# Linear attention and a highway feed-forward on one core: feed-forward in token rows, keys and queries turned in 64-row tiles

## The chip, the core and the metric

The kernel runs on one core of a Trainium2 chip. The metric is the device time of one execution in microseconds. Three executions of the kernel before took 109.54 (median), 109.30 and 109.64 us.

## What is computed

Linear attention with a decay per head, over 4 batches, 8 heads, 768 positions and head size 64, followed by a highway layer over 3,072 tokens of width 512. From the reference (blocks of 64 positions):

```python
intra = einsum('bhic,bhjc->bhij', qb, kb) * Dmask
intra = einsum('bhij,bhjd->bhid', intra, vb)
inter = einsum('bhid,bhde->bhie', qb * lam_pow, kv_state)
out[:, :, sl] = intra + inter
kv_state = lam_block * kv_state + einsum('bhsd,bhse->bhde', kb * rev_pow, vb)
...
H = maximum(x @ w_h, 0);  T = sigmoid(x @ w_t + b_t)
return T * H + (1 - T) * x
```

`x` is the attention output as token rows of 512 features. The inputs and the output are float32.

## The kernel before

A step n is 256 positions of one batch with all heads; there are 12 steps, three per batch, each of two halves b of 128 positions. The decay is folded into queries and values: the query is multiplied by a power of lambda, the value by its inverse, so that the running state `kv`, a PSUM bank, needs no decay.

The order of all work is written out by hand in the string PLAN. Each token names an operation, its step and parts, sometimes an engine (`@ACT`) and the PSUM banks that it takes (`=40`). All engines work through their tokens in that order. The seven banks b0 to b6 each hold one tile at a time; the eighth is `kv`. BUFS gives the number of buffers of each SBUF tile.

For each step: `Lk`, `Lq`, `Lv` load halves of the heads on SyncE's queue (L173), in packets of 512 bytes (two positions of 64 floats). `CK` casts the keys, `CQ` and `CV` scale queries and values (L190); `TK` and `TQ` turn keys and queries in 128x128 transposes (L204), 16 for a step; `EK` and `EQ` copy them out as kT and qT (L101 on ScalarE, L103 on VectorE and GpSimd). `SS` interleaves the scores (L216) with the update of the state (L221); `KE` copies the state out. `M` masks the scores on VectorE (L255). `I` and `A` add state part (L271) and masked part (L281) into a bank bo, whose columns are tokens and whose partitions are features; `D` copies it out as xT.

The feed-forward works on xT with features in the partitions. `F` holds a 128x128 piece of a weight matrix and streams 256 tokens (L300), 32 matmuls for a step, fewer tokens in the last. `H` computes max(h, 0) - x (L305), `G` the sigmoid with the bias as a column (L314), `X` the product th (L318), all with features in the partitions. `R` turns x and th back to token rows in PSUM and adds them there, by matmuls with the identity in 64-row tiles (L347; L327 for the last step), `E` copies the sum out and `ST` stores it (L356, L337). `Z` issues spins, matmuls on zeros that fill waiting time of TensorE in the opening (L366).

The lines that a reader needs for the tile shapes:

```python
T.transpose(t[:, i, j, :], get(x + "b", n)[:, j, h:h + 2, :], id128)                # 128x128
T.matmul(get("x", n, r)[:, b, j, :], lhsT=x[half(r), j, b * C:(b + 1) * C],
         rhs=id128[half(r), half(r)], ...)                                          # 64-row tiles
```

Of the kernel before, what the change touches and what calls it, by code (L numbers as in the profile page):

```python
# [17 lines left out]
Lk.0.0 Lv.0.1 Lv.0.0 Lq.0.0 Lk.0.1 Lq.0.1 Lv.1.1 CK.0.0@POOL Lq.1.0 Z.12=0 TK.0.0=0 Lq.1.1 CV.0.0@DVE Lk.1.0  # L18
CQ.0.0@POOL EK.0.0@DVE Lv.1.0 CV.0.1@DVE CK.0.1@ACT Lk.1.1 Z.11=1 TQ.0.0=1 B=2 EQ.0.0@ACT CQ.0.1@POOL W.0.1 W.0.0
Z.6=0 TQ.0.1=3 TK.0.1=4 EQ.0.1@DVE U.0.0 EK.0.1@ACT W.1.1 S.0.0=56 KE.0.0@DVE S.0.1=01 CQ.1.2@POOL W.1.0 M.0.0.1 Z.1=3  # L20
U.0.1 I.0=34 M.0.1.1 KE.0.1@ACT Lk.2.1 M.0.0.0 A.0.1 M.0.1.0 TQ.1.2=0 Lq.2.1 CV.1.2@DVE CK.1.2@ACT EQ.1.2@ACT Lq.2.0
Z.8=1 TK.1.2=1 A.0.0 EK.1.2@DVE Lk.2.0 D.0.0@DVE Z.3=5 SS.1.1=56 WC.0.0.1@ACT WC.0.0.0@POOL M.1.1.0 KE.1.0@ACT
WC.0.1.0@POOL D.0.1@ACT Lv.2.1 WC.0.1.1@DVE Z.4=0 SS.1.0=01 M.1.1.1 I.1=35 KE.1.1@ACT Lv.2.0 F.0.0.0=4 WC.1.1.0@DVE PT
M.1.0.1 Lk.3.1 F.0.1.0=6 M.1.0.0 WC.1.0.0@POOL WC.1.0.1@ACT Lk.3.0 WC.1.1.1@DVE A.1.1 A.1.0 BC F.0.0.1=1 H.0.1 Lq.3.1
D.1.1@ACT H.0.0 D.1.0@ACT F.0.1.1=0 Lq.3.0 CQ.2.2@POOL F.1.0.0=2 Lv.3.0 G.0.1@ACT CK.2.2@DVE F.1.0.1=6 Lv.3.1
G.0.0@ACT X.0.1@DVE TQ.2.2=5 Lq.4.0 X.0.0@DVE TK.2.2=4 EQ.2.2@ACT CV.2.2@POOL F.1.1.0=3 Lq.4.1 EK.2.2@DVE G.1.0@ACT
H.1.0 SS.2.0=01 Lk.4.1 H.1.1 CK.3.2@POOL SS.2.1=54 Lk.4.0 M.2.0.1 F.1.1.1=2 KE.2.0@ACT M.2.1.0 Lv.4.0 TK.3.2=3 M.2.1.1
CQ.3.2@POOL G.1.1@ACT I.2=15 M.2.0.0 Lv.4.1 A.2.1 X.1.0@DVE A.2.0 Lk.5.0 R.0=40 D.2.0@ACT D.2.1@DVE CV.3.2@POOL
TQ.3.2=6 E.0.0@ACT Lk.5.1 F.2.1.1=1 E.0.1@ACT EQ.3.2@DVE Lq.5.1 EK.3.2@ACT X.1.1@DVE F.2.1.0=5 CQ.4.2@POOL Lq.5.0
R.1=40 H.2.1 SS.3.1=62 Lv.5.0 F.2.0.0=3 CK.4.2@POOL KE.3.0@ACT M.3.1.1 Lv.5.1 E.1.1@ACT M.3.1.0 SS.3.0=52 E.1.0@ACT  # L30
H.2.0 Lq.6.0 TQ.4.2=0 KE.3.1@ACT CV.4.2@POOL M.3.0.1 TK.4.2=6 G.2.1@ACT Lq.6.1 F.2.0.1=4 M.3.0.0 EQ.4.2@ACT EK.4.2@DVE
Lv.6.0 I.3=32 A.3.0 CK.5.2@POOL A.3.1 Lk.6.1 SS.4.1=56 D.3.0@ACT D.3.1@DVE TK.5.2=0 KE.4.0@ACT M.4.1.1 Lk.6.0
F.3.0.0=2 G.2.0@ACT CQ.5.2@POOL EK.5.2@DVE Lv.6.1 SS.4.0=36 H.3.0 F.3.0.1=0 Lq.8.0 M.4.0.0 CV.5.2@POOL M.4.0.1
TQ.5.2=2 Lk.9.0 G.3.0@ACT F.3.1.0=3 X.2.1@DVE Lq.7.0 EQ.5.2@ACT X.2.0@DVE F.3.1.1=6 CQ.6.2@POOL M.4.1.0 Lq.7.1
KE.4.1@ACT I.4=14 H.3.1 G.3.1@ACT R.2=25 Lk.8.1 X.3.0@DVE A.4.0 E.2.1@ACT X.3.1@DVE A.4.1 Lk.7.1 SS.5.0=30 E.2.0@ACT
D.4.0@DVE CK.6.2@POOL SS.5.1=56 D.4.1@ACT Lk.7.0 TQ.6.2=2 M.5.0.0 KE.5.0@ACT CV.6.2@POOL TK.6.2=1 M.5.1.1 Lv.7.0
EQ.6.2@ACT F.4.1.0=4 M.5.0.1 Lv.7.1 EK.6.2@ACT F.4.0.0=3 H.4.1 Lk.8.0 M.5.1.0 I.5=62 SS.6.1=01 H.4.0 Lq.8.1 A.5.0
KE.6.0@ACT M.6.1.0 CQ.7.2@POOL R.3=45 Lv.9.1 A.5.1 M.6.1.1 SS.6.0=30 D.5.0@ACT Lv.8.0 F.4.0.1=1 M.6.0.0 D.5.1@ACT
M.6.0.1 Lk.9.1 TQ.7.2=6 G.4.0@ACT CK.7.2@POOL F.5.0.0=3 Lq.10.1 EQ.7.2@ACT F.4.1.1=2 H.5.0 Lk.10.1 E.3.1@ACT X.4.0@DVE
TK.7.2=0 CV.7.2@POOL G.4.1@ACT I.6=63 ST.0 KE.6.1@DVE F.5.0.1=5 X.4.1@DVE Lv.8.1 F.5.1.0=1 G.5.0@ACT CK.8.2@POOL  # L40
EK.7.2@DVE Lq.9.0 A.6.0 E.3.0@ACT H.5.1 A.6.1 SS.7.1=20 Lq.9.1 D.6.0@ACT D.6.1@DVE TK.8.2=4 M.7.1.1 F.6.1.0=1 Lv.9.0
EK.8.2@ACT X.5.0@DVE CK.9.2@POOL F.6.1.1=6 KE.7.0@DVE Lk.10.0 CQ.8.2@POOL H.6.1 R.4=30 SS.7.0=54 Lk.11.1 E.4.0@ACT
F.5.1.1=1 E.4.1@ACT M.7.0.1 G.6.1@ACT ST.4 M.7.1.0 TK.9.2=3 Lq.10.0 M.7.0.0 TQ.8.2=0 G.5.1@ACT CV.8.2@POOL F.6.0.0=4
EQ.8.2@DVE Lk.11.0 KE.7.1@ACT X.5.1@DVE I.7=25 EK.9.2@ACT Lq.11.0 A.7.0 H.6.0 A.7.1 CQ.9.2@POOL SS.8.0=01 X.6.1@DVE
D.7.1@ACT Lv.10.1 SS.8.1=34 M.8.0.1 D.7.0@ACT F.6.0.1=6 KE.8.0@DVE Lq.11.1 CK.10.2@POOL F.7.0.0=5 M.8.1.0 G.6.0@ACT
M.8.1.1 ST.3 TQ.9.2=1 CV.9.2@POOL H.7.0 F.7.1.0=2 EQ.9.2@ACT Lv.10.0 X.6.0@DVE TK.10.2=3 M.8.0.0 ST.1 I.8=45
EK.10.2@ACT CQ.10.2@POOL H.7.1 SS.9.1=61 A.8.1 KE.9.0@ACT M.9.1.0 A.8.0 R.5=02 M.9.1.1 SS.9.0=36 CK.11.2@POOL
E.5.1@DVE F.7.0.1=1 KE.9.1@ACT M.9.0.1 E.5.0@ACT F.7.1.1=2 D.8.0@DVE D.8.1@ACT ST.5 CQ.11.2@POOL M.9.0.0 G.7.0@ACT
Lv.11.1 TK.11.2=6 Lv.11.0 I.9=04 F.8.1.0=5 EK.11.2@ACT ST.2 X.7.0@DVE TQ.10.2=3 G.7.1@ACT H.8.1 CV.10.2@POOL F.8.0.0=1
EQ.10.2@ACT R.6=65 H.8.0 A.9.1 X.7.1@DVE A.9.0 SS.10.1=31 D.9.0@ACT D.9.1@DVE F.8.1.1=2 E.6.1@ACT M.10.1.1 F.9.1.0=0  # L50
E.6.0@DVE G.8.1@ACT M.10.1.0 ST.6 TQ.11.2=4 CV.11.2@POOL KE.10.0@DVE F.9.1.1=5 EQ.11.2@ACT X.8.1@DVE SS.10.0=16
G.9.1@ACT H.9.1 R.7=32 M.10.0.1 KE.10.1@ACT F.8.0.1=4 X.9.1@DVE E.7.0@ACT M.10.0.0 E.7.1@ACT I.10=06 SS.11.0=53
G.8.0@ACT ST.7 A.10.0 M.11.0.0 A.10.1 SS.11.1=21 D.10.1@ACT X.8.0@DVE F.9.0.0=5 KE.11.0@ACT M.11.1.0 D.10.0@ACT
F.9.0.1=6 M.11.0.1 M.11.1.1 F.10.1.0=4 G.9.0@ACT H.9.0 I.11=20 X.9.0@DVE A.11.0 A.11.1 R.8=31 D.11.0@ACT R.9=56
E.8.0@ACT F.10.0.0=2 E.9.0@DVE E.9.1@ACT E.8.1@ACT D.11.1@DVE ST.9 F.10.1.1=3 H.10.0 ST.8 F.10.0.1=6 H.10.1 G.10.1@ACT
F.12.1.1=5 G.10.0@ACT X.10.1@DVE F.11.1.1=1 F.11.1.0=0 G.12.1@ACT X.10.0@DVE F.11.0.1=2 G.11.1@ACT H.11.1 F.12.1.0=4
R.10=36 G.11.0@ACT H.12.1 X.11.1@DVE F.11.0.0=0 E.10.0@ACT X.12.1@DVE F.12.0.1=4 E.10.1@ACT H.11.0 F.12.0.0=1
G.12.0@ACT X.11.0@DVE ST.10 R.11.1.1=5 H.12.0 R.11.0.2=3 E.11.1.1@DVE X.12.0@DVE E.11.0.2@ACT ST.11.1.1 R.11.1.0=0
ST.11.0.2 E.11.1.0@DVE ST.11.1.0
"""  # L60

BUFS = dict(kf=5, qf=5, vf=5, kb=3, qb=2, vs=3, kT=2, qT=2, m=8, xT4=2, th4=2, xT2=3, xT1=2, th2=2, th1=2, hm2=3, hm1=2, tb2=2, tb1=2, ss=4, o=5, oh=2, oq=1)
# [3 lines left out]
def kernel(  # L66
# [18 lines left out]
    J = 2  # L85
    N = B * NST
# [19 lines left out]
    lam_bc = singles.tile([128, H], F32)  # L106
    A.dma_start(out=lam_bc, in_=lam.partition_broadcast(128))
    bt_r = singles.tile([KC, 128], F32)
    A.dma_start(out=bt_r, in_=moe_b_t.rearrange("(j p) -> j p", p=128))
    id128 = singles.tile([128, 128], BF16)  # L110
    make_identity(nc, id128)
    blank = singles.tile([128, 512], BF16)
    V.memset(blank, 0.0)
    tk_i = singles.tile([128, NST, J], I32)
    P.iota(tk_i, pattern=[[2 * C, NST], [1, J]], base=0, channel_multiplier=J)
    tri = singles.tile([128, J, J, C // J], F32)
    P.memset(tri, 1.0)
    for b in range(2):
        P.affine_select(out=tri[half(b)], in_=tri[half(b)], compare_op=ALU.is_ge, fill=0.0, base=0,
                        pattern=[[-1, J], [1, J], [J, C // J]], channel_multiplier=-J)  # L120
    tri = tri.rearrange("p j i q -> p j (i q)")
    tk_f = singles.tile([128, NST, J], F32)
    V.tensor_copy(tk_f, tk_i)
    id_f = singles.tile([KC, KC], F32)
    V.tensor_copy(id_f, id128[0:KC, 0:KC])
    A.preload_act_table_set("natural_log_exp_and_others")
    ln_bc = singles.tile([128, H], F32)
    A.activation(ln_bc, lam_bc, AF.Ln)
    p_ln = singles.tile([128, NST, H, J], F32)
    V.tensor_tensor(p_ln, in0=ln_bc[:, None, :, None].to_broadcast([128, NST, H, J]),  # L130
                    in1=tk_f[:, :, None, :].to_broadcast([128, NST, H, J]), op=ALU.mult)
    pow_q = singles.tile([128, NST, H, J], F32)
    A.activation(pow_q, p_ln, AF.Exp)
    pow_v = singles.tile([128, NST, H, J], F32)
    A.activation(pow_v, p_ln, AF.Exp, scale=-1.0)
    bt_col = singles.tile([128, KC], F32)
# [4 lines left out]
    kv = ps.tile([128, NP, 128], F32, tag="kv", name="kv", bufs=1)  # L141
    V.memset(kv, 0.0)


    made = {}

    def groups(n, b):
        return ((n,), b) if n < N - 1 else ((n, b), 0)
# [12 lines left out]
    def get(*key):  # L161
        return made[key]
# [7 lines left out]
    def load(x, n, p, eng):  # L170
        b, c = divmod(n, NST)
        hs = heads(p)
        (A if eng else nc.sync).dma_start(out=new((x + "f", n), [128, H, J * D], F32)[:, hs],  # L173
                          in_=SRC[x][b, hs, c * 2 * C:(c + 1) * 2 * C, :].rearrange("h (p j) d -> p h (j d)", j=J))

# [7 lines left out]
    def cast_k(n, p, eng):  # L183
        hs = heads(p)
        copy(eng, new(("kb", n), [128, J, H, D])[:, :, hs].rearrange("p j h d -> p h j d"),
             get("kf", n)[:, hs].rearrange("p h (j d) -> p h j d", j=J))

    def scale(n, p, eng, src, dst, pw):
        z = H if p == 2 else 4
        ENG[eng].tensor_tensor(dst, in0=get(src, n)[:, heads(p)].rearrange("p h (j d) -> p h j d", j=J),  # L190
                               in1=pw[:, n % NST, heads(p), :, None].to_broadcast([128, z, J, D]), op=ALU.mult)

    def cast_q(n, p, eng):
        scale(n, p, eng, "qf", new(("qb", n), [128, J, H, D])[:, :, heads(p)].rearrange("p j h d -> p h j d"), pow_q)

    def cast_v(n, p, eng):
        scale(n, p, eng, "vf", new(("vs", n), [128, H, J, D])[:, heads(p)], pow_v)

# [220 lines left out]
```

## Time and profile before

| | us |
|---|---|
| median of three runs | 109.54 |
| span of the profiled execution, the only time that its record gives | 109.3 |
| TensorE, matmuls busy | 99.4 |
| VectorE busy | 82.7 |
| ScalarE busy | 71.9 |
| GpSimd busy | 55.7 |
| share of the 16 DMA engines, loads and stores | 85.1% |

The span runs from the first to the last instruction. Matmuls overlap, so a busy TensorE need not be at its peak; the chain of waits tells better what a block of matmuls costs. GpSimd's times are rough. Engines wait for each other through semaphores, and the profile names the one that came last.

### The profile page before, as it was taken

How to read it: one execution, taken by the hardware profiler on the slowest of the kernel's cores; microseconds unless marked ns; L12 is line 12 of the kernel's file. 1: busy time of each engine (PE TensorE's matmuls, PEld its weight loads, DVE VectorE, ACT ScalarE, POOL GpSimd, SP SyncE). 2: the span in 40 equal slices, each digit the busy share in tenths (PEclk: the TensorE clock that was granted, in tenths of full speed). 3: DMA queues.
4: the chain of work that ended last, by engine and by line, in shares of the span. 5: the costliest groups of instructions: out<-in, count | busy, mean ns of one | idle time of the engine just before them, and what ended most of it. 6: DMA issues, size and time to landing. Idle time of an engine off the chain costs nothing.

```text
span 109.3 us, 4968 instructions
## 1 busy us (share of the span) xinstructions
PE 99.4 (91%) x2188; PEld 80.6 (74%) x2190; DVE 82.7 (76%) x140; ACT 71.9 (66%) x129; POOL 55.7 (51%) x46
## 2 busy tenths in 40 slices
PE   4986989899999999999999999998999599999950
PEld 1343654688887878889899889896888478899940
DVE  1241595878998696999977989999858958958960
ACT  3304263787866489499579749975696758776940
POOL 6029420427979858959468296499691600000000
PEclk9999999999999999999999999999999999999999
DMA  0899999999999999989999999599999413207264
GB/s 5 233 304 290 291 366 386 312 290 287 290 266 304 287 250 262 302 228 289 296 300 293 305 341 270 181 346 326 321 333 323 170 69 125 73 6 296 94 233 151
DMA packets 42701, 27.59 MB, mean 252 GB/s; under 512 B 1588, under 2 KB 38712, under 8 KB 42680
## 3 DMA queue, kind: packets, MB, share of 16 engines
q1 hardware_dynamic: 42528, 27.27, 85.1%
q8 instruction: 17, 0.28, 1.2%
q14 instruction: 4, 0.03, 0.1%
q10 hardware_dynamic: 152, 0.01, 0.1%
HBM read 20.98 MB, written 6.29 MB: 249 GB/s over the span
## 4 chain that ended last, share of the span: by engine, by line
PE 61%; DMA 11%; DVE 6%; POOL 5%; ACT 5%; issue 4%; SPq 4%; POOLq 0%; DVEq 0%
PE bt L300 15%; PE bh L300 13%; DMA qf<-in_q_dram 11%; PE bs L216 7%; PE bo L281 5%; PE bx L347 5%; PE bspin L366 4%; PE bqtr L204 4%; DVE m L255 3%; SPq L173 3%; PE bktr L204 3%; POOL qb L190 3%; PE bo L271 3%; ACT qT L101 2%; POOL vs L190 2%
## 5 line engine op out<-in xcount | busy, mean ns | idle before, releaser
L300 PEld LDWEIGHTS <-w_b 128*128 128x128 bf16 x416 | 36.3, 98 | 6.4 <-issue 1.8
L255 DVE TENSOR_TENSOR m<-bs,tri 128x512 bf16<-128x512 f32 x48 | 31.1, 682 | 3.8 <-PE bs L216 3.4
L190 POOL TENSOR_TENSOR qb<-qf,pow_q 128x1024 bf16<-128x1024 f32 (+1 forms) x13 | 23.6, 1813 | 11.2 <-DMA qf<-in_q_dram 10.6
L314 ACT ACTIVATE bt<-bt,bt_col 128x256 f32<-128x256 f32 (+1 forms) x52 | 22.0, 432 | 6.9 <-PE bt L300 4.2
L300 PE MATMUL bt<-xT,w_b 128*128 128x256 bf16 (+1 forms) x208 | 24.5, 265 | 1.3 <-ACT qT L101 1.3
L300 PE MATMUL bh<-xT,w_b 128*128 128x256 bf16 (+1 forms) x208 | 25.0, 265 | 0.2 <-issue 0.2
L190 POOL TENSOR_TENSOR vs<-vf,pow_v 128x1024 bf16<-128x1024 f32 x10 | 19.0, 1904 | 5.0 <-DMA vf<-in_v_dram 4.6
L305 DVE SCALAR_TENSOR_TENSOR hm<-bh,xT 128x512 bf16<-128x512 f32 (+1 forms) x26 | 16.5, 643 | 4.0 <-PE bh L300 2.5
L318 DVE TENSOR_TENSOR th<-bt,hm 128x512 bf16<-128x512 f32 (+1 forms) x26 | 16.5, 643 | 2.1 <-ACT bt L314 2.0
L216 PE MATMUL bs<-qT,kT 64*64 64x128 bf16 x384 | 14.2, 218 | 0.6 <-issue 0.3
L101 ACT ACTIVATE xT<-bo 128x512 bf16<-128x512 f32 x16 | 11.5, 749 | 4.6 <-PE bo L281 4.6
L103 POOL CAST kb<-kf 128x1024 bf16<-128x1024 f32 (+1 forms) x10 | 10.0, 995 | 8.1 <-DMA kf<-in_k_dram 6.8
L101 ACT ACTIVATE ss<-kv 128x512 bf16<-128x512 f32 x15 | 8.9, 595 | 7.3 <-PE bs L216 6.1
L366 PE MATMUL bspin<-blank,id 128*128 128x512 bf16 x43 | 11.8, 416 | 1.6 <-POOL id masks.py:199 1.4
L216 PEld LDWEIGHTS <-kT 64*64 64x64 bf16 x384 | 11.0, 106 | 2.9 <-issue 1.4
L101 ACT ACTIVATE o<-bx 128x512 f32<-128x512 f32 x19 | 10.4, 596 | 1.4 <-PE bx L347 1.3
L101 ACT ACTIVATE qT<-bqtr 128x1024 bf16<-128x1024 bf16 (+1 forms) x10 | 9.8, 980 | 1.8 <-PE bqtr L204 1.8
L281 PE MATMUL bo<-m,vs 64*64 64x128 bf16 x384 | 9.4, 219 | 0.7 <-DVE m L255 0.4
L221 PE MATMUL kv<-vs,kb 64*64 64x64 bf16 x320 | 9.2, 196 | 0.2 <-POOL vs L190 0.2
L366 PEld LDWEIGHTS <-id 128*128 128x128 bf16 x45 | 4.3, 105 | 6.4 <-issue 1.7
L204 PE MATMUL bqtr<-id,qb 128*128 128x128 bf16 x96 | 7.5, 220 | 0.9 <-POOL qb L190 0.9
L281 PEld LDWEIGHTS <-vs 64*64 64x64 bf16 x384 | 6.6, 106 | 2.4 <-issue 1.5
(50 smaller groups left out, 109.1 us busy)
## 6 DMA issues: line engine op xcount, KB each, us to landing
kf<-in_k_dram SPq DMA_DIRECT2D x24, 256.0 KB, 5.5
vf<-in_v_dram SPq DMA_DIRECT2D x24, 256.0 KB, 5.4
qf<-in_q_dram SPq DMA_DIRECT2D x24, 256.0 KB, 5.5
out_dram<-o SPq DMA_DIRECT2D x11, 512.0 KB, 4.7
w_f<-in_moe_w_h_dram SPq DMA_DIRECT2D x2, 512.0 KB, 6.6
w_f<-in_moe_w_t_dram SPq DMA_DIRECT2D x2, 512.0 KB, 8.5
out_dram<-oh SPq DMA_DIRECT2D x2, 128.0 KB, 2.0
out_dram<-oq SPq DMA_DIRECT2D x1, 256.0 KB
```

Of the source, the lines that this page charges most:

```text
L101: A.activation(dst, src, AF.Copy)
L103: ENG[eng].tensor_copy(dst, src)
L190: ENG[eng].tensor_tensor(dst, in0=get(src, n)[:, heads(p)].rearrange("p h (j d) -> p h j d", j=J), in1=pw[:, n % NST, heads(p), :, None].t ...
L204: T.transpose(t[:, i, j, :], get(x + "b", n)[:, j, h:h + 2, :], id128)
L216: T.matmul(get("s", n, e, hp // 2)[half(b), hp % 2, j, :], lhsT=get("kT", n)[half(e), hp, j, half(b)], rhs=get("qT", n)[half(e), hp, :, ha ...
L255: V.tensor_tensor(new(("m", n, e, u), [128, 2, J, C]), in0=get("s", n, e, u), in1=tri[:, None].to_broadcast([128, 2, J, C]), op=ALU.mult)
L281: T.matmul(get("o", n, b)[half(e), hp, :], lhsT=get("vs", n)[half(b), 2 * hp + e, j, :], rhs=get("m", n, e, u)[half(b), hp % 2, j, :], sta ...
L300: T.matmul(t[:, r, :], lhsT=w_b[w][:, kc, (2 * u + r) * 128:(2 * u + r + 1) * 128], rhs=get("xT", *g)[:, kc, :], start=(kc == 0), stop=(kc ...
L305: V.scalar_tensor_tensor(new(("hm", g, u), [128, 2, z * C], tag=f"hm{z}"), in0=get("h", g, u), scalar=0.0, in1=get("xT", *g)[:, 2 * u:2 * ...
L314: A.activation(dst[:, r, :], src[:, r, :], AF.Sigmoid, bias=bt_col[:, 2 * u + r:2 * u + r + 1])
L318: ENG[eng].tensor_tensor(new(("th", g), [128, NP, z * C], tag=f"th{z}")[:, 2 * u:2 * u + 2, :], in0=get("tt", g, u), in1=get("hm", g, u), ...
L366: T.matmul(t, lhsT=id128, rhs=blank, start=True, stop=True)
```

## The change

The feed-forward now works in token rows. `F` holds 128 tokens of xT and streams 512 columns of a weight matrix, so that the result has tokens in the partitions. The bias is written into the bank of the gate by a copy on ScalarE or VectorE (`BP`) before the matmuls add to it; it is spread over 128 partitions once (`B`, `BB`, `BC`), from a sum of three bfloat16 parts. x is turned once, in whole 128x128 transposes (`TX`), and copied out in bfloat16 (`XC`). `H`, `G` and `X` then give the same expressions in float32 token rows, and a new `Y` adds x on VectorE or GpSimd; its result is stored. `R` and `E` are gone.

Keys and queries are turned by one token `T` from step 2 on (the third), in 32 matmuls of 64-row tiles into two banks; `FK` and `FQ` copy each half out. Steps 0 and 1 keep whole transposes. The query is loaded differently: eight positions of one head in a partition, in packets of 2,048 bytes, with the even heads in one load and the odd ones in the other, and its powers are laid out to match. The opening has another order of loads, and lambda is spread by small matmuls. The order PLAN is new throughout. Some stores are split at row 119. `load_wc`, `cast_wc` and `scores_state_intra` are defined and not used by PLAN.

```diff
+    for r in range(3):
+        A.dma_start(out=b_f[32 * r:32 * r + 1], in_=moe_b_t.rearrange("(o f) -> o f", o=1))
...
+        if x == "q":
+            nc.sync.dma_start(out=new(("qf", n), [128, 2, Q * D], F32)[:, p],
+                              in_=q[b].rearrange("(h e) (c p j) d -> c e p h (j d)", e=2, p=C // NP, j=Q)[c, p])
+            return
...
+    def turned(x, n, i):
+        if x == "k":
+            return get("kb", n)[:, i % J, 2 * (i // J):2 * (i // J) + 2, :]
+        return get("qb", n)[:, i]
...
+    def trans_rows(n, bk):
+        for r in range(2):
+            bank(("tr", n, r), bk[r], [128, 2, 8, 64], BF16)
+        for i, x in enumerate("kq"):
+            for c in range(8):
+                for r in range(2):
+                    T.transpose(get("tr", n, r)[:, i, c, :], turned(x, n, c)[half(r)], id128[half(r), half(r)])
+
+    def evac_k_rows(n, r, eng):
+        copy(eng, new(("kT", n), [128, NP, J, C])[:, :, :, half(r)].rearrange("e h j p -> e (h j) p"), get("tr", n, r)[:, 0])
+
+    def evac_q_rows(n, r, eng):
+        copy(eng, new(("qT", n), [128, NP, 2 * C])[:, :, r * C:(r + 1) * C].rearrange("e h (p j) -> e h p j", j=Q),
+             get("tr", n, r)[:, 1].rearrange("e j (p h) -> e h p j", h=NP))
...
-    def block(i, u, w, bk):
-        g, z = group(i)
-        t = bank(("ht"[w], g, u), bk[0], [128, 2, z * C])
-        for r in range(2):
-            for kc in range(KC):
-                T.matmul(t[:, r, :], lhsT=w_b[w][:, kc, (2 * u + r) * 128:(2 * u + r + 1) * 128],
-                         rhs=get("xT", *g)[:, kc, :], start=(kc == 0), stop=(kc == KC - 1))
+    def rows(n, p, bk):
+        bs = range(2) if p == 2 else (p,)
+        t = bank(("x", n, p), bk[0], [C, len(bs), KC, 128], BF16)
+        for i, b in enumerate(bs):
+            for j in range(KC):
+                T.transpose(t[:, i, j, :], get("xT", n)[:, j, b * C:(b + 1) * C], id128)
...
+    def block(n, b, w, p, bk):
+        z = cols(p)
+        t = get("t", n, b, p) if w else bank(("h", n, b, p), bk[0], [C, z.stop - z.start])
+        for j in range(KC):
+            T.matmul(t, lhsT=get("xT", n)[:, j, b * C:(b + 1) * C], rhs=w_b[w][:, j, z], start=(j == 0 and not w), stop=(j == KC - 1),
+                     skip_group_check=True)
+
+    def begin(n, b, p, eng, bk):
+        z = cols(p)
+        t = bank(("t", n, b, p), bk[0], [C, z.stop - z.start])
+        if eng:
+            copy(eng, t, b_bc[:, z])
...
+    def relu(n, b, p):
+        z = cols(p)
+        V.scalar_tensor_tensor(new(("y", n, b), [C, DM], F32)[:, z], in0=get("h", n, b, p), scalar=0.0,
+                               in1=get("xr", n, b)[:, z], op0=ALU.max, op1=ALU.subtract)
+
+    def sigm(n, b, p):
+        z = cols(p)
+        A.activation(new(("g", n, b), [C, DM], F32)[:, z], get("t", n, b, p), AF.Sigmoid)
+
+    def gate(n, b, p, eng):
+        z = cols(p)
+        y = get("y", n, b)[:, z]
+        ENG[eng].tensor_tensor(y, in0=y, in1=get("g", n, b)[:, z], op=ALU.mult)
+
+    def total(n, b, p, eng):
+        z = cols(p)
+        o = new(("o_sb", n), [C, 2, DM], F32, tag="ob")[:, b, z]
+        ENG[eng].tensor_tensor(o, in0=get("y", n, b)[:, z], in1=get("xr", n, b)[:, z], op=ALU.add)
```

How many operations each engine has, from PLAN: the feed-forward has 46 `F` of four 512-column matmuls and 4 of four 256-column ones; `X` and `Y` are 15 and 17 on GpSimd, 10 and 8 on VectorE; `XC` 4 on ScalarE and 9 on VectorE; `BP` 22 on ScalarE and 3 on VectorE; `G` 25 on ScalarE; `FK` 9 and `FQ` 17 on ScalarE, 11 and 3 on VectorE; spins 28, and 4 more ahead of PLAN.

## Prediction

> **What bounds the kernel now.** First the page: busy shares and slices.
>
> ```profile
> span 109.3 us, 4968 instructions
> ...
> PE 99.4 (91%) x2188; PEld 80.6 (74%) x2190; DVE 82.7 (76%) x140; ACT 71.9 (66%) x129; POOL 55.7 (51%) x46
> ...
> DMA  0899999999999999989999999599999413207264
> ```
>
> TensorE leads, VectorE is second, and the DMA engines are full up to about 85 us. Shares are averages, so next the table of windows, which shows each stage (columns: length, then busy us and count of PE, PEld, DVE, ACT, POOL, clock, DMA share, GB/s):
>
> ```profile
> 45.00:50.00 5.00, 5.00 (x138) 4.59 (x140) 5.00 (x10) 4.02 (x8) 3.86 (x3) 1.00 0.95 267
> 55.00:60.00 5.00, 5.00 (x98) 4.58 (x95) 3.59 (x6) 4.45 (x8) 3.71 (x4) 1.00 1.14 295
> 85.00:90.00 5.00, 3.74 (x92) 3.05 (x90) 3.71 (x7) 3.20 (x6) 1.78 (x1) 1.00 0.33 120
> ```
>
> PE is full in most windows at clock 1.00; the one visible hole is at 85 to 90, where the chain of waits comes from a q transfer (DMA, POOL qb, ACT qT). DVE can be full (45 to 50), but over the twelve windows from 25 to 85 it sums to 52.3 of 60 us, 87%. The chain of waits gives what PE blocks really cost, one behind the other (start, us, what):
>
> ```profile
> 36.55 0.57 PE bx L347 x32
> ...
> 40.25 0.45 PE bktr L204 x8
> ...
> 51.38 1.75 PE bh L300 x16
> ```
>
> So 32 matmuls in 64-row tiles take 0.57 us, 8 whole 128-column transposes 0.45 (0.056 each), a 256-column matmul 0.109. Last, groups by form (count, busy, mean ns) for the other engines:
>
> ```profile
> L318 DVE TENSOR_TENSOR th<-bt,hm 128x512 bf16<-128x512 f32 x22 | 14.9, 684 | 2.0 <-ACT bt L314 2.0
> L314 ACT ACTIVATE bt<-bt,bt_col 128x256 f32<-128x256 f32 x44 | 19.5, 449 | 6.7 <-PE bt L300 4.2 <-ACT xT L101 0.9 <-ACT o L101 0.8
> L101 ACT ACTIVATE o<-bx 128x512 f32<-128x512 f32 x19 | 10.4, 596 | 1.4 <-PE bx L347 1.3
> L190 POOL TENSOR_TENSOR qb<-qf,pow_q 128x512 bf16<-128x512 f32 x2 | 2.6, 1310 | 2.3 <-DMA qf<-in_q_dram 2.3
> L103 DVE COPY kT<-bktr 128x1024 bf16<-128x1024 bf16 x5 | 3.4, 685 | 1.2 <-PE bktr L204 1.1
> L103 DVE COPY kT<-bktr 128x512 bf16<-128x512 bf16 x1 | 0.4, 418 | 0.0
> ```
>
> Queued DVE instructions overlap by some 0.06 us: the chain has four masks in 2.48 us, so I count 0.62 for a mean of 0.685 and 0.37 for one of 0.42. With these, all DVE instructions of before sum to 82.6, the page's 82.7.
>
> **TensorE, part by part.**
> - Feed-forward: 352 matmuls of 256 columns and 64 of 128 (42.0 us) become 184 of 512 and 16 of 256. From 0.056 and 0.109 a line gives 0.217 at 512: 41.7, so -0.3 (-0.1 if just doubled, -1.0 without any fixed part). Weight loads fall from 416 to 200 and stay hidden.
> - Turning back: 11 blocks of 0.57 and 16 matmuls of 0.056 (7.2) become 96 transposes of 0.056 (5.4): -1.8.
> - Keys and queries: 192 transposes (10.75) become 32 (1.8) and ten blocks of 32 in 64-row tiles (5.7, by the bx row, the same tile shape): -3.3.
> - Changes of tile shape: in the trace the step from L271 to L281 takes 149 ns where 56 is usual, from L300 to L347 205 where 109 is; some 95 ns each. In program order there are 59 such changes before and 65 after: +0.6. The one bias matmul: +0.2.
> Sum -4.6. Spins (45 to 28, and 4 cold ones) only fill waits: nothing. Scores, states, intra and inter are unchanged.
>
> **VectorE.** Out: 26 gates (15.1), five evacuations of bx (2.6), kT and qT copies (5.1), three state copies (1.9), one weight cast (0.4). In: 18 of the 50 gates and sums (16 x 0.62 + 2 x 0.37 = 10.7), nine copies of the turned x (5.3), 11 of the kT halves, 3 of the qT halves and one opening kT (5.8), three bias copies (1.9), queries scaled for three steps and a half (4.1), more of values and keys (1.3), the splitting of the bias (2.3), setup (0.8). Relu and masks stay. Net +7, to 89.6. So DVE becomes the fullest engine.
>
> **ScalarE.** 52 sigmoids (22.1) become 25, of 512 columns without a bias column, 0.60 to 0.69 each; 20 output copies go; 22 bias copies into the bank come (0.6 each by row o, 12.7), four turned x, 29 half and 2 whole copies of kT and qT for 2 and 15, six key casts for two. By row means, less the overlap that before shows (71.9 busy for 75.8 of means), 71.9 becomes about 82. The bias copy is a new wait: PE's gate matmul stands behind it, and everything later on PE with it. It is issued ahead of that matmul in the queue, so I take nothing; uncovered it costs 0.5 to 0.6 each, 12 us over 22.
>
> **GpSimd.** 32 gates and sums come, four full query and value scalings and five key casts go. The opening shows the price twice:
>
> ```profile
> 8.04 0.68 DVE L190 TENSOR_TENSOR vs<-vf,pow_v 128x512 bf16<-128x512 f32 x1
> 8.05 1.58 POOL L190 TENSOR_TENSOR qb<-qf,pow_q 128x512 bf16<-128x512 f32 x1 [2.11 <-DMA qf<-in_q_dram]
> ...
> 9.78 1.04 POOL L190 TENSOR_TENSOR qb<-qf,pow_q 128x512 bf16<-128x512 f32 x1 [0.16 <-DMA qf<-in_q_dram]
> ```
>
> The same operation took 1.04 us with DVE idle and 1.58 beside a DVE operation on two SBUF tensors, which was not slower itself. Other POOL work sums to 45; 30 full operations at 1.04 give 77, and at most 25 meetings with such DVE operations add 0.54 each, 90. I take 80, for meetings are partial; off the path with 20 us to spare. The Trainium skill, "GPSIMD Engine Reference", section 1, says that GpSimd shares its SBUF interfaces with VectorE and contends with DVE instructions on two SBUF inputs, and section 4.1 gives two-input work to VectorE as about 2x faster. The two rows agree; by that rule alone all 30 would be at 1.58 and POOL at 93.
>
> **DMA.** q now comes in 2,048-byte rows. In the trace's packets 512 bytes took 30.2 ns in the mean and 2,048 bytes 88.2: 12,288 of the first (371 us of one engine) become 3,072 of the second (271): -100/16 = -6.3 us of the 93 that 85.1% mean. Loads should end near 78 instead of 85, so they can follow a faster PE. Stores are 20 issues for 14 on SP, whose queue waited 24 us for results in before. Most are queued behind the last loads, ten of 1.4 us of DMA in about 16: covered, barely.
>
> **Opening and tail.** The first mask is at 13.28. After: k, q, q, k lead, the small lam transfer no longer goes to 128 partitions; but DVE has the bias splitting ahead of its share of the query. Counting from landings of before (5.3, then about 0.9 apart): bias split to 8, query 8.7, key 9.6, kT 10, value 10.7, mask 11 to 13.3; I take 12.0. Tail: sigmoid, gate, sum, store for sigmoid, gate, matmul, copy, store; 3.05 us from the last engine operation to the end stay.
>
> **The sum.** PE alone: 109.3 - 4.6 - 1.3 = 103.4. DVE: 82.1 us of its work lie behind the first mask (89.6 less setup, bias and the first half casts, 7.5). It filled 87% when another engine paced and 99% in its best windows; as the pacing engine I take 92%: 12.0 + 82.1/0.92 + 3.05 = 104.3. The later one counts. The median, 109.54, lies 0.2 over the profiled span: **104.5 us**.
>
> **Rivals.**
> - *DVE paces, no better filled than now* (ends slower). Before, from first mask to last copy, it is busy 78.1 of 93.0 us, 84%. Masks, relu, gates, sums and turned-x copies share one in-order queue, and a wait for ACT or POOL in front holds the mask that PE needs. At 84%: 12 + 97.7 + 3.05 + 0.2 = 113. It decides below 87% (82.1 in 94.3). For it: 87% is the mean of 25 to 85; ACT and POOL are fuller too. Against: windows at 5.00.
> - *Everything falls into place*: opening at 11, and the holes of 70 to 90 us close (PE misses 1.8 us there) since loads are 6.3 us ahead: 109.5 - 4.6 - 2.3 - 1.8 = 100.8. For it: full DVE windows; against: it needs DVE at 95%.
> - *POOL ends last*: 12 gates and sums stand on POOL after the last step's inter; at 1.58 they take 19 us for DVE's 13, so the end comes 3 later, 107.5. The sharing rule of the Trainium skill's "GPSIMD Engine Reference", section 1, describes this mechanism.
> - *The 64-row tiles don't run side by side*, the change not doing what it says: ten blocks then cost 0.9 as now, 3.3 come back: 106.8. Against: the bx row.
>
> **Chances.** Forecast 0.45 (its own range 102 to 107.5), all in place 0.18, POOL 0.10, tiles 0.03, DVE slower 0.24. A difference of 0.3% is about what a measurement can tell here. Within it lie 0.02 of POOL and 0.02 of the slower case: faster 0.74, same 0.04, slower 0.22. From 100.0 to 110.5 about 0.03 is left out below and 0.16 above.
>
> **What would show it.** Right: DVE near 90 us busy and above 90% of its stretch, PE blocks of turned keys and queries at 0.57, ten of them, first mask near 12, DMA clear by 78. Wrong: DVE under 87% between masks with PE waiting for masks or bias copies; POOL near 90 with the last sums on it; a first mask after 13.

## The result, and the profile after

The changed kernel took 122.92 us (median of four, 121.64 to 123.58) beside 109.42 us for the kernel before on the same chip: a ratio of 1.120, with a 95% interval of 1.113 to 1.128. The forecast was 104.5 us and its range ended at 110.5, so both are wrong, and so is the sign. A few executions of a kernel run longer at a lower granted clock; the ratios leave them out, so a median can lie above what its ratio says.

The page of the changed kernel (busy shares, then three rows of the 40 slices):

```profile
span 121.3 us, 4341 instructions
...
PE 98.9 (82%) x1831; PEld 60.7 (50%) x1853; DVE 101.1 (83%) x157; ACT 74.7 (62%) x131; POOL 89.2 (74%) x72
...
POOL 7256076326019999999999999993979959957780
PEclk9999999995999999999999999855999999999996
```

VectorE is the fullest engine, as forecast, but with 101.1 us instead of 89.6; GpSimd is at 89.2, the upper end of its bounds, and full without a break from 40 to 80 us; TensorE was granted half its clock for two stretches of the work, 3.4 us from 27.0 on and 6.8 us from 78.2 on. The windows show the same stage by stage (length, busy us and count of PE, PEld, DVE, ACT, POOL, clock, DMA share, GB/s); the last row is the stretch from the first mask to VectorE's last operation:

```profile
75.00:80.00 5.00, 1.65 (x82) 1.36 (x82) 2.22 (x4) 1.50 (x4) 4.92 (x4) 0.82 0.96 302
...
77.00:78.00 1.00, 0.00 (x0) 0.00 (x0) 0.00 (x0) 0.00 (x0) 0.92 (x2) 1.00 0.84 258
...
80.00:85.00 5.00, 4.62 (x52) 3.37 (x53) 4.53 (x8) 3.39 (x7) 2.99 (x3) 0.50 0.25 77
...
12.64:118.16 105.52, 88.51 (x1761) 55.62 (x1782) 92.03 (x136) 69.38 (x122) 82.48 (x55) 0.95 0.75 226
```

VectorE worked 92.0 of 105.5 us, 87.2%, where the forecast had 82.1 us at 92%. From 77 to 78 only GpSimd works. The chain of waits says what is behind it (start, us, what):

```profile
72.55 2.34 POOL vs L245
74.89 1.44 POOL kb L115
76.33 1.22 POOL y L422
...
77.64 1.15 POOL ob L427
...
78.82 0.69 DVE y L412
79.51 0.61 DVE xT L115
...
80.17 1.00 PE btr L265 x31
```

VectorE's relu (`H.6.1`, y L412) needs one of the four y buffers. It started at 78.82, when GpSimd had ended the sum `Y.5.1` (ob L427, from 77.64), which reads and so holds such a buffer and stands in GpSimd's in-order queue behind scalings, a cast and a gate. Behind the relu in VectorE's queue stands `D.7.0` (xT L115), which frees the bank that `T.9` (btr L265) takes. So TensorE stood still for 3.2 us, from 76.92 to 80.17, and its clock was 0.50 from 78.2 to 85.0. The first low clock, from 27.0 to 30.4, follows 1.7 us in which TensorE waited for nothing that the profile shows; that hole stays unexplained.

The groups by form show the second half of the loss (count, busy, mean ns, idle before):

```profile
L342 DVE TENSOR_TENSOR m<-bs,tri 128x512 bf16<-128x512 f32 x48 | 30.9, 682 | 3.7 <-PE bs L285 2.4 <-PE kv L290 1.0
L427 DVE TENSOR_TENSOR ob<-y,xs 128x512 f32<-128x512 f32 x7 | 9.7, 1383 | 0.1
L422 DVE TENSOR_TENSOR y<-y,g 128x512 f32<-128x512 f32 x9 | 8.6, 964 | 0.2
...
L427 POOL TENSOR_TENSOR ob<-y,xs 128x512 f32<-128x512 f32 x16 | 20.3, 1280 | 1.1 <-DVE y L422 0.6
```

Masks, with one operand in PSUM, take 682 ns as before, and none of the 48 more than 693, however busy GpSimd was. VectorE's sums and gates, with both in SBUF, take 1383 and 964 ns in the mean. The gates of before took 684: ScalarE wrote the sigmoid back into its bank there, and the gate read PSUM. The change moved that operand to SBUF.

**Where the difference lies.** From the forecast span of 104.3: more VectorE work behind the first mask, (92.0 - 82.1)/0.92 = 10.8; less filled, 92.0/0.872 - 92.0/0.92 = 5.5; first mask at 12.64 instead of 12.0, 0.6; tail 0.1. Sum 121.3, as measured. Outside the span lie 1.7 us, not the 0.2 that the forecast took: the eleven executions of before that stand beside the last runs below have spans of 106.7 to 107.9 for 108.69 to 109.90 us, so the profiled execution of before, with its span of 109.3, was a longer one.

### The profile page after: what moved, and what is told of

The parts are those of the page before. It is cut to its first block, busy times and chain, and to the rows that moved or that the text cites. A ratio compares the mean times of both kernels' runs of the same rounds, so it can differ in the third digit from the quotient of the medians.

```text
span 121.3 us, 4341 instructions
## 1 busy us (share of the span) xinstructions
PE 98.9 (82%) x1831; PEld 60.7 (50%) x1853; DVE 101.1 (83%) x157; ACT 74.7 (62%) x131; POOL 89.2 (74%) x72
## 4 chain that ended last, share of the span: by engine, by line
PE 36%; DVE 33%; POOL 15%; issue 9%; ACT 3%; DVEq 0%; POOLq 0%; ACTq 0%
DVE m L342 9%; PE bh L399 8%; DVE y L412 6%; PE bt L399 6%; POOL ob L427 5%; PE bspin L457 5%; DVE y L422 5%; PE bs L285 5%; POOL vs L245 3%; POOL y L422 3%; DVE ob L427 3%; PE bo L364 3%; DVE vs L245 3%; POOL kb L115 2%; PE btr L265 2%
## 5 line engine op out<-in xcount | busy, mean ns | idle before, releaser
L422 POOL TENSOR_TENSOR y<-y,g 128x512 f32<-128x512 f32 (+1 forms) x15 | 20.7, 1386 | 12.9 <-ACT g L417 9.4
L399 PEld LDWEIGHTS <-xT 128*128 128x128 bf16 x200 | 18.2, 99 | 18.8 <-issue 2.6
L399 PE MATMUL bt<-w_b,xT 128*128 128x512 bf16 (+1 forms) x91 | 24.4, 378 | 1.6 <-ACT bt L113 0.8
L399 PE MATMUL bh<-w_b,xT 128*128 128x512 bf16 (+1 forms) x91 | 24.1, 377 | 0.6 <-issue 0.2
L427 POOL TENSOR_TENSOR ob<-y,xs 128x512 f32<-128x512 f32 (+1 forms) x17 | 21.0, 1247 | 1.2 <-DVE y L422 0.6
L245 POOL TENSOR_TENSOR vs<-vf,pow_v 128x1024 bf16<-128x1024 f32 (+1 forms) x10 | 19.6, 1959 | 2.0 <-DMA vf<-in_v_dram 2.0
L412 DVE SCALAR_TENSOR_TENSOR y<-bh,xs 128x512 f32<-128x512 f32 (+1 forms) x25 | 16.4, 663 | 5.4 <-POOL ob L427 3.2
L417 ACT ACTIVATE g<-bt 128x512 f32<-128x512 f32 (+1 forms) x25 | 14.6, 585 | 7.0 <-PE bt L399 6.8
L113 ACT ACTIVATE bt<-b_bc 128x512 f32<-128x512 f32 (+1 forms) x22 | 12.6, 587 | 6.1 <-DVE y L412 5.8
L113 ACT ACTIVATE ss<-kv 128x512 bf16<-128x512 f32 x18 | 10.8, 601 | 8.3 <-PE kv L290 4.6
L427 DVE TENSOR_TENSOR ob<-y,xs 128x512 f32<-128x512 f32 (+1 forms) x8 | 10.4, 1306 | 0.1
```

The source lines that it names most:

```text
L113: A.activation(dst, src, AF.Copy)
L245: ENG[eng].tensor_tensor(new(("vs", n), [128, H, J, D])[:, heads(p)], in0=get("vf", n)[:, heads(p)].rearrange("p h (j d) -> p h j d", j=J) ...
L399: T.matmul(t, lhsT=get("xT", n)[:, j, b * C:(b + 1) * C], rhs=w_b[w][:, j, z], start=(j == 0 and not w), stop=(j == KC - 1), skip_group_ch ...
L412: V.scalar_tensor_tensor(new(("y", n, b), [C, DM], F32)[:, z], in0=get("h", n, b, p), scalar=0.0, in1=get("xr", n, b)[:, z], op0=ALU.max, ...
L417: A.activation(new(("g", n, b), [C, DM], F32)[:, z], get("t", n, b, p), AF.Sigmoid)
L422: ENG[eng].tensor_tensor(y, in0=y, in1=get("g", n, b)[:, z], op=ALU.mult)
```

## The experiments

The first question was which of four things costs the time: the y buffers, the load on VectorE with what GpSimd does to it, the bias copies, or the tiles. "y = 8" below means the changed kernel with eight y buffers. Ratios are to the kernel before.

| run | us | ratio (95%) | span | DVE | POOL |
|---|---|---|---|---|---|
| changed | 122.92 | 1.120 (1.113 to 1.128) | 121.3 | 101.1 | 89.2 |
| e1: y = 8 | 118.50 | 1.087 (1.082 to 1.093) | 116.8 | 102.4 | 89.5 |
| e2: GpSimd's gates and sums cut | 113.66 | 1.042 (1.031 to 1.054) | 111.4 | 97.5 | 62.8 |
| e3: all gates and sums on VectorE | 138.03 | 1.252 (1.243 to 1.262) | 137.6 | 121.9 | 49.8 |
| e4: all biases by matmul | 124.56 | 1.142 (1.134 to 1.149) | 122.9 | 103.0 | 88.4 |
| e6: y = 8, g = 4, gates on VectorE in bfloat16 | 120.32 | none | 118.2 | 104.3 | 67.7 |
| e7: y = 8, whole transposes | 118.21 | 1.068 (1.058 to 1.079) | 116.2 | 102.3 | 89.0 |
| e8: e6, and copies moved off VectorE | 124.48 | 1.131 (1.122 to 1.141) | 124.2 | 95.5 | 67.7 |
| e9: y = 8 without VectorE's gates | 112.29 | 1.026 (1.021 to 1.030) | 111.4 | 91.9 | 86.0 |
| e10: y = 8 without GpSimd's gates | 115.34 | 1.050 (1.045 to 1.055) | 112.8 | 99.3 | 66.2 |
| e11: y = 8, all sums on GpSimd | 121.23 | 1.105 (1.100 to 1.109) | 118.5 | 94.6 | 96.9 |
| e14: y = 8, six gates read PSUM | 116.40 | 1.059 (1.052 to 1.066) | 116.1 | 100.8 | 86.1 |
| e5: before with tiles in ten steps | 118.00 | 1.071 (1.064 to 1.078) | 116.5 | 84.1 | 55.7 |
| e12: before with tiles in three steps | 116.41 | 1.060 (1.054 to 1.066) | 110.8 | 82.8 | 55.5 |
| e15: e5 with whole transposes | 114.05 | 1.045 (1.040 to 1.050) | 112.4 | 82.6 | 55.6 |

Spans and busy times are of the one profiled execution. For e6 no ratio is on record. e2, e3 and e4 have four y buffers, like the changed kernel.

**The buffers.**

```diff
-BUFS = dict(... y=4, g=3, ob=5)
+BUFS = dict(... y=8, g=3, ob=5)
```

> The tile y gets 8 buffers instead of 4, nothing else. In the changed kernel VectorE's relu of step 6 waits 2.8 us for a sum on GpSimd that frees its y buffer, and the turning block of TensorE stands still for 3.3 us behind it, after which the clock is at half. Theory 'buffers': these waits are the loss; they go, the clock stays near 1.00, and the time falls by 5 us or more, to 117 or less. Theory 'full queue': GpSimd is full from 45 to 80 us and its sums are late anyway; whoever waits for them (stores, the scaled values of the next steps) only waits elsewhere, and the time stays within 2 us of 123.

Measured: 118.50, so 4.4 us, between the two theories' ranges. Over the same stretch as above, first mask to VectorE's last operation, the window is

```profile
12.46:113.69 101.23, 88.72 (x1794) 53.77 (x1782) 93.53 (x136) 69.64 (x123) 83.11 (x55) 0.98 0.79 236
```

VectorE is filled to 93.5/101.2 = 92.4%, the share that the forecast had, where the changed kernel has 87.2%; its busy time did not fall. The buffers explain the hole, and with it the worse filling, but no more than a third of the loss of 13.5.

**GpSimd's share of the gates and sums.** In e2 its operations touch 16 columns (a memset fills the rest of the sum, and that part is not computed), in e3 they move to VectorE (`X.*@DVE`, `Y.*@DVE`), in e10 and e9 the gates of one engine are dropped from PLAN.

```diff
 def gate(n, b, p, eng):
     z = cols(p)
+    if eng == "POOL":
+        z = slice(z.start, z.start + 16)
```

> The gates and sums that PLAN gives to GpSimd are cut to 16 of their columns, and the rest of the sum is a memset to zero: this part of the output is not computed. Theory 'GpSimd and the shared interface': GpSimd falls from 89 to about 60 us busy; the sums on VectorE, 1.38 us now, go to about 0.69, so VectorE falls from 101 to about 91; the stretch from first mask to end shortens to what VectorE needs, 82 to 85 us at 92 to 87%, and the time is 106 to 112. Theory 'VectorE's own count paces': the interface gives little back, VectorE stays above 97 busy and the time above 117. Theory 'bias copies on ScalarE hold TensorE': GpSimd does not matter, time above 119.

> All gates and sums on VectorE, none on GpSimd, whole computation. GpSimd falls to about 48 us busy, VectorE gets 32 operations more. If the interface is what stretches VectorE's operations on two SBUF tensors, each goes to about 0.69 and VectorE's busy time is 101 - 11 + 20 = about 110, and as the fullest engine it gives 118 to 126 us, so that moving work between the two gains nothing. If they stay at 0.9 to 1.4 with GpSimd idle, the length is their own (float32 output), VectorE reaches about 125 busy and the time is over 132.

> The same, but GpSimd's fifteen gates are left out and VectorE's ten stay. GpSimd loses 20 of 89 us, VectorE at most 3 us of contention. Theory 'VectorE paces': 114.5 to 118 us. Theory 'GpSimd paces': it is full from 45 to 85 us, where some 12 of these gates lie; 106 to 111.

> The changed kernel with 8 y buffers, where the ten gates that PLAN gives to VectorE are left out (their product is not computed); GpSimd's fifteen stay. VectorE loses about 9 of 102 us. Theory 'VectorE paces, filled to 88%': the span falls by 9/0.88, from 118.5 to 107 to 110 us. Theory 'GpSimd paces' or 'the order holds it': 116 or more.

Measured: 113.66, 138.03, 115.34 and 112.29. e2 came out between its theories: VectorE fell to 97.5, not to 91, and its sums still took 1126 ns, since GpSimd kept its scalings; VectorE was 92% filled with four y buffers, so the run relieves these too. Against e1, dropping GpSimd's gates took 23 us of work from GpSimd and none from VectorE's queue, yet VectorE's busy time fell by 3.1 us and the time by 3.2. Dropping VectorE's own ten gates took 10.5 us off VectorE and 6.2 off the time, less than the 8.5 to 11.5 expected, and GpSimd got 3.5 us shorter. So the two engines lengthen each other, and VectorE's length sets the end. By its time alone e3 speaks for the other theory, that the length is the operations' own; its trace does not. With GpSimd left with casts and scalings only, the groups of e3 are

```profile
L427 DVE TENSOR_TENSOR ob<-y,xs 128x512 f32<-128x512 f32 x23 | 22.3, 982 | 0.2
...
L422 DVE TENSOR_TENSOR y<-y,g 128x512 f32<-128x512 f32 x23 | 21.6, 948 | 1.2 <-ACT g L417 0.8
```

far above 690 still. But 15 of the 25 sums and 12 of the 25 gates met no GpSimd operation, and all of these took 0.68 to 0.69 (0.42 at 256 columns). Of the 23 that met one, 14 were lengthened, up to 2.39; the other nine kept 0.68 to 0.69, having started first or at the same time, or just before GpSimd's end, or beside a scaling that was itself drawn out to 4.41 or 6.83 from its 1.90.

**The pairs by themselves.** That the lengthening goes with GpSimd's operations was a reading so far. e13 runs the changed kernel, and behind it, with everything else quiet, rows of 128x512 operations:

```diff
+def v_two(): V.tensor_tensor(dv, in0=i0, in1=i1, op=ALU.add)     # two SBUF tensors
+def v_bank(): V.tensor_tensor(dv, in0=pt, in1=i1, op=ALU.add)    # pt lies in PSUM
+def v_one(): V.tensor_copy(dv, i0)
+def g_two(): P.tensor_tensor(po, in0=p0, in1=p1, op=ALU.add)
```

> The whole changed kernel runs first; behind it stand eight short stretches on VectorE and GpSimd alone, with no DMA, no TensorE and no ScalarE beside them, each a row of 128x512 operations: VectorE sums of two SBUF tensors alone; GpSimd sums of two SBUF tensors alone; both together; VectorE sums with one operand in PSUM beside GpSimd sums; VectorE copies of one SBUF tensor beside GpSimd sums; VectorE bfloat16 sums beside GpSimd float32 sums; VectorE two-tensor sums, and then sums with a PSUM operand, beside GpSimd casts. The total time means nothing. Theory (a VectorE operation that reads two SBUF tensors waits while a GpSimd operation is on the way, and one that reads PSUM does not): 0.68 alone, a mean of 1.2 to 2.4 beside GpSimd's sums, 0.68 with the PSUM operand; GpSimd 1.04 alone, 1.1 to 1.6 in the pairs. Rival (what lengthens is any SBUF access under load, transfers included): the two-tensor sums stay at 0.68 to 0.8 in these quiet stretches. Second rival (GpSimd slows every VectorE operation): the PSUM form and the one-tensor copy lengthen as well.

The timeline of e13 (start, us, what): two-tensor sums alone on VectorE; alone on GpSimd; both; PSUM form beside GpSimd's sums; copies beside them:

```profile
119.98 4.31 DVE L515 TENSOR_TENSOR dv<-i,i 128x512 f32<-128x512 f32 x6
...
124.68 7.96 POOL L519 TENSOR_TENSOR po<-p,p 128x512 f32<-128x512 f32 x6
...
132.88 11.55 DVE L515 TENSOR_TENSOR dv<-i,i 128x512 f32<-128x512 f32 x8
...
133.56 9.59 POOL L519 TENSOR_TENSOR po<-p,p 128x512 f32<-128x512 f32 x6
...
144.74 7.99 POOL L519 TENSOR_TENSOR po<-p,p 128x512 f32<-128x512 f32 x6
144.78 7.21 DVE L516 TENSOR_TENSOR dv<-pt,i 128x512 f32<-128x512 f32 x10
...
152.97 10.34 DVE L517 COPY dv<-i 128x512 f32<-128x512 f32 x10
```

Alone, one takes 0.72 from start to start on VectorE and 1.33 on GpSimd. Together they alternate, one of each in 1.67: VectorE's operation takes 1632 ns, GpSimd's 1588. With one operand in PSUM VectorE keeps 0.72 and GpSimd 1.33, as if the other weren't there. The float32 copy, 0.43 when it meets nothing, takes 1.37 in the row; the bfloat16 sum also 1.37, and 0.43 behind GpSimd's last. Beside GpSimd's casts the two-tensor sum takes 0.98 and the cast 0.95; the PSUM form 0.69 and the cast 0.61. The first operation of VectorE in the third row, already on its way when GpSimd began, took 0.68, and GpSimd's next one waited. The theory holds and both rivals fall; it was too narrow in one point, since a fast copy of one SBUF tensor waits as well.

The Trainium skill, "SBUF — State Buffer", "Who interferes with whom", states this as a lock: VectorE's second pair of SBUF ports is GpSimd's only one, two SBUF inputs or a copy in a two-port mode take it, who issues first keeps it for the instruction, and a VectorE instruction with at most one SBUF input outside those modes doesn't contend. The runs agree on who contends and on the order of issue. On the other blocking fully they are not decisive: one strictly after the other would be 0.72 + 1.33 = 2.05 for a pair, and it took 1.67. In the row each operation ends 0.55 (VectorE) or 1.12 us (GpSimd) after the end of the other, 0.14 less than it takes alone, so all but 0.14 us of each waits; what these 0.14 are, no run shows.

**The same in the kernel.** In e14 the sigmoid stays in its bank for six of VectorE's gates, and two sums read the gate's result there (the count in the expectation, seven and three, is too high):

```diff
+if (n, b) in INB: A.activation(get("t", n, b, p), get("t", n, b, p), AF.Sigmoid)
...
+V.tensor_tensor(t if (n, b) in SUMB else y, in0=y, in1=t, op=ALU.mult)
```

> The changed kernel with eight y buffers, and for seven of VectorE's ten gates the sigmoid is written back into its PSUM bank, so that the gate reads one operand from PSUM; for three of them the gate's result stays in the bank too, so that the sum reads PSUM. Nothing leaves or joins an engine. Theory (contention for the SBUF interfaces lengthens VectorE's two-tensor operations): these ten operations take 0.68 each (half for 256 columns) in place of 10.0 us together as in the kernel with eight buffers alone, VectorE's busy time falls by 2.5 to 3.5 us and the time from 118.5 to about 115 to 116.5. Rival (the lengthening only shifts to the other two-tensor operations, because GpSimd is full all the same): busy time within 1 us of 102.4 and the time within 1 us of 118.5. Rival (the bank is held longer, and TensorE waits for it): the time rises.

The groups of e14; the sums of the last line kept both operands in SBUF:

```profile
L429 DVE TENSOR_TENSOR y<-y,bt 128x512 f32<-128x512 f32 x4 | 2.7, 685 | 0.3
...
L437 DVE TENSOR_TENSOR ob<-bt,xs 128x512 f32<-128x512 f32 x2 | 1.4, 686 | 0.0
...
L439 DVE TENSOR_TENSOR ob<-y,xs 128x512 f32<-128x512 f32 x5 | 7.7, 1542 | 0.0
```

All eight take 0.69. In e1's trace four of them had taken 2.21, 1.18, 1.53 and 1.30, and the other four 0.68 to 0.73, so 3.5 us were there to win. Busy time fell by 1.6 us on VectorE, less than the 2.5 to 3.5 expected, since other operations met GpSimd instead (the three full gates left in SBUF took 1.34 in the mean, in e1 0.78), and by 3.4 on GpSimd. The ratio fell from 1.087 to 1.059, and the intervals lie apart: the edit, the place of one operand of eight operations, was worth some 3 us (0.028 of 109). It also takes load off the three g buffers; no run separates the two. Of the versions of the changed kernel that compute everything this is the nearest to the kernel before, and none beat it.

**Other loads.** e4 writes every bias by a matmul (`BP.n.b.p=bank` without an engine), e6 puts all gates on VectorE with y and g in bfloat16 and a fourth g buffer, e8 adds to this `XC@ACT`, `D@ACT` and biases by matmul, e11 puts all sums on GpSimd.

> The bias goes into the bank by a matmul of ones with the three parts instead of a copy on ScalarE or VectorE: 25 copies less (ScalarE -12.7, VectorE -2 us), 25 matmuls more on TensorE (+5.4 us). Theory 'bias copies hold TensorE': ScalarE waited 5.8 us before them and TensorE behind them; time falls by 4 us or more. Theory 'VectorE and GpSimd pace': TensorE has room, nothing on the pacing engines changes but three copies; time within 2 us of 123.

> The changed kernel with 8 y buffers and 4 g buffers, y and g in bfloat16, and all gates on VectorE; the sums stay where they are. GpSimd loses 15 gates of 1.4 us (89.5 to about 68 busy); VectorE gets 15 more, and if two bfloat16 operands go at twice the rate, all 25 take about 0.42 instead of 0.95. Theory 'GpSimd and the shared interface': 112 to 116 us, against 118.5 with the buffers alone, and VectorE's sums come down from 1.58. Theory 'VectorE's count': 25 gates on VectorE for 10, so 119 or more.

> All remedies that the theory points to: 8 y buffers, bfloat16 y and g, all gates on VectorE, the turned x and the attention result copied out by ScalarE alone, the bias written by a matmul. VectorE falls to about 90 us busy, GpSimd to about 68, ScalarE stays near 75, TensorE gets 5.4 us. Theory 'VectorE and GpSimd pace': 106 to 112 us. Rival 'the order of the queues, not the load, holds it': 115 or more although no engine is above 95 us busy.

> The changed kernel with 8 y buffers and all sums on GpSimd: eight leave VectorE, which loses 11 to 12 us with the contention in them; GpSimd gets 10 and reaches 99 busy. The whole computation. Theory 'VectorE paces': 107 to 112 us as long as GpSimd ends in time. Theory 'both are needed': GpSimd takes over as the last engine, 116 to 120.

e4: ScalarE fell from 74.7 to 64.2 and the time rose by 1.6: the bias copies were no loss. e6: a bfloat16 gate took 0.42 alone, but up to 1.37 beside GpSimd, VectorE ended at 104.3, and nothing was won. e8: no engine above 102.1 and still 124.48; GpSimd waited 36.5 us for VectorE's gates. This fits the rival of its expectation, that the order written out by hand, made for other owners, holds the time; the run is no measure of the loads. e11: VectorE fell to 94.6, and GpSimd, at 96.9, ended last. So neither engine can take all of the new work.

**The tiles.** e7 turns keys and queries in 16 whole transposes, keys in one bank and queries in the other. e5 does the reverse: the kernel before with `T`, `FK`, `FQ` in steps 2 to 11, e12 in steps 2, 4 and 6, and e15 is e5 with whole transposes in the same places.

```diff
-    bank(("tr", n, r), bk[r], [128, 2, NP, J, 64], BF16)          # e5: a bank holds 64 rows of keys and of queries
+    bank(("tr", n, i), bk[i], [128, NP, J, C], BF16)              # e15: a bank holds keys, or queries
```

> The changed kernel with 8 y buffers, where T turns keys and queries in 16 whole 128-column transposes, keys in one bank and queries in the other, copied out by the same halves. TensorE gets about 3.3 us more over ten steps. Theory 'VectorE and GpSimd pace': hidden, 117.5 to 119.5 us, as with the buffers alone. Theory 'TensorE still paces behind the holes': 121 or more.

> One part of the change alone: the kernel before, where keys and queries from step 2 on are turned together in 64-row tiles into two banks and copied out by halves; query layout, feed-forward and all else as before. Theory 'the term was right and only covered by other engines in the changed kernel': TensorE paces this kernel and has 3.3 us less to do, less 0.1 for each further change of tile shape; 106 to 108 us. Rival 'the tiles do not pay': ten more copies' fixed costs on ScalarE and VectorE and the turning moved to the later of its two places cost as much, or the 64-row blocks take 0.9 us; 109 or more.

> The kernel before with 64-row tiles in steps 2, 4 and 6 only, where the two turnings stand close together in the order and little is moved. TensorE: 3 x (1.0 - 0.62) = 1.1 us less. Theory 'the tiles are worth their time where TensorE paces': 108 to 109, 0.5 to 1% faster. Theory 'copies by halves eat it': same or slower, 109.5 to 111.

> The kernel before, with keys and queries of steps 2 to 11 turned in one place and copied out by halves exactly as in the kernel of the run with the tiles in before, but in whole 128x128 transposes, keys in one bank and queries in the other. If the tiles themselves lost the time there: 109.4 to 112. If the place and the copies by halves lost it, as the copies on its chain suggest: 117 to 119, within 1 us of 118.0 or up to 3 us above it, since a block of 32 tiles is 0.3 us shorter than 16 whole transposes.

e7: 118.21 against 118.50, and by the ratios even 1.068 against 1.087, with the intervals apart. So the tiles save nothing in the changed kernel, where VectorE paces, and may cost some 2 us; which of the two figures holds stays open. e5: 118.00, where 3 us less of TensorE work could have shown. The twin e15 took 114.05, with the same order and the same halved copies, between the two ranges of its expectation. So the place and the copies cost about 4.5%, of which the cause in detail stays open, and the tiles another 2.6%, although a block of tiles is shorter. Waits of TensorE in e5 (total us, times, longest):

```profile
PE bx L319 <- ACT qT L60: 1.5, 1, 1.5
...
PE bo L253 <- DVE kT L62: 1.3, 1, 1.3
PE bs L188 <- ACT qT L60: 1.2, 5, 0.3
PE bh L272 <- ACT qT L60: 1.1, 1, 1.1
PE bh L272 <- DVE qT L62: 1.1, 1, 1.1
...
PE bs L188 <- DVE kT L62: 0.5, 2, 0.2
```

That is 6.7 us of waiting for copies of kT and qT, and 2.4 in e15's list (0.8, 0.7, 0.5 and 0.4): 4.3 more, and the spans differ by 4.1. Each bank of tiles holds half of the keys and half of the queries, so it comes free only after both copies, and the next user on TensorE (bh, bo, bx) waits. e12 is inconclusive, and outside both ranges of its expectation: its six executions scatter from 112.78 to 119.04, and in the profiled one TensorE stood for 2.0 us at 57.5 for nothing that the profile shows.

## Why the prediction was wrong, point by point

- **VectorE's durations** (the term "Net +7, to 89.6"). This step failed. The counts were right; the sums and gates were priced at 0.62 because gates with a PSUM operand had that price, and meetings with GpSimd were priced at nothing on VectorE's side. Measured against the prices of operations that met nothing (0.69, casts 0.42; 1024 columns taken as twice 512): sums 5.2 us too much, gates 2.5, value scalings 1.7, key casts 1.4, the bias split 0.7: 11.5 together, as much as 101.1 - 89.6.
- **The reading of the opening.** The prediction saw the 1.58 beside VectorE and concluded that VectorE "was not slower itself". In that row VectorE started at 8.04 and GpSimd at 8.05. e13 shows that this order decides: the one on its way keeps its price. One row in one order was taken for both.
- **GpSimd at 80.** The term was mis-sized: 89.2. Besides the meetings, its shortest full gates take 1.26 and its shortest full sums 1.15 in the changed kernel, not the 1.04 of the scaling that writes bfloat16. And "off the path with 20 us to spare" was the wrong question: a full in-order queue holds y buffers long before it ends last.
- **92% filled.** Measured 87.2%, and 92.4% with eight buffers (e1). So a pacing VectorE does fill better, as the prediction argued, and the term failed through the y buffers, which it didn't count. The rival "VectorE paces, no better filled than now" had its 87%, but its 113 was made with the same 82.1 us of work. Its 78.1 of 93.0 us in the kernel before is 78.8 by the windows, 85%, which changes nothing.
- **First mask.** 12.64 for 12.0, and not after 13:

```profile
11.60 1.12 DVE L245 TENSOR_TENSOR vs<-vf,pow_v 128x512 bf16<-128x512 f32 x1
12.64 1.28 DVE L342 TENSOR_TENSOR m<-bs,tri 128x512 bf16<-128x512 f32 x2
```

In the opening VectorE's bias piece took 1.44, its key cast 1.26 and its value scaling 1.12, all beside GpSimd, some 2 us over their prices alone. The mask followed the value scaling at once, so the same cause had a part in the delay; how much of it, no run shows.
- **TensorE.** Right in its sizes at full clock, but nothing was gained by them (e7, e5). Four 512-column matmuls are 0.86 to 0.87 in the chain, so 0.217 each, and a block of tiles 0.57:

```profile
90.52 0.57 PE btr L265 x32
```

- **DMA.** 0.749 of 121.3 is 90.9 us, so some -2, not -6.3: the packets of 2,048 bytes took 99.2 ns in the mean instead of 88.2. No wait for a transfer stands in the chain of the hole.
- **ScalarE.** 74.7 us instead of about 82, without effect on the time as far as e4 shows.
- **Bias copies at nothing, tail 3.05.** Right: taking the bias copies off gained nothing (e4); and 121.3 - 118.16 = 3.1.
- **Other rivals.** "GpSimd ends last" is what e11 makes true, not the change itself. "The tiles don't run side by side" is false by the row above.

## What to carry to other kernels

Before an elementwise step is moved from PSUM operands to SBUF operands, count how many of VectorE's operations will read only SBUF while GpSimd is busy, and price each that comes behind a running GpSimd operation at what is left of that operation plus its own length; leaving one operand in its bank avoided it here. An operation that starts first keeps its price, and GpSimd's then waits. Work given to GpSimd comes back as VectorE time in this way, and through buffers that wait in its queue. A contention price read from one row has to be read for both orders of start.

## What was not expected of the hardware

A VectorE operation with an operand in PSUM kept 0.69 beside GpSimd's sums and casts, one with two in SBUF took 1.63 in a row beside sums that take 1.26 alone, and a pair cost 1.67 where each alone takes 0.72 and 1.33. A plain float32 copy within SBUF waited likewise, 0.43 becoming 1.37. TensorE's clock was granted at 0.50 for 3.4 and 6.8 us after two holes of 1.7 and 3.2 us; the Trainium skill, "TensorE: Matmul & The Clock Gate", "Part 1: The HAM clock gate", names windows of about 3.4 us for both directions. The lengths of the slow stretches agree, one window and two, but both falls came sooner than an idle window after TensorE had stopped, 1.7 and 1.3 us after it.
